# A gated state-space and attention kernel: score, maxima and convolution tiles of the second half drawn from three PSUM tiles in turn, with a new list of steps and edits to head, passage and tail

## The chip, the cores and the metric

The kernel runs on one core of a Trainium2 chip. The metric is the device time of one execution in microseconds (us); before the change the median of three runs is 784.46 us (779.76 to 787.62).

## What is computed

Input `x` is 2048 x 448. The output mixes two branches by a gate per row:

```python
g = sigmoid((x * gate_w).sum(-1, keepdims=True))
out = g * a + (1 - g) * b
# a: state-space convolution; 448 channels, 256 complex states each
A = -exp(log_A_real) + 1j * A_imag;  dt = exp(log_dt)
K = 2 * einsum("dn,dnl->dl", (C_real + 1j * C_imag) * dt[:, None], exp(A * dt * pos)).real
a = irfft(rfft(x, 4096) * rfft(K, 4096))[:2048] + x * D_skip
# b: 16 heads of 28 columns, 4 segments of 512 rows, causal softmax inside a segment
p = softmax(q @ k.T * scale + mask)
o = sigmoid(beta) * (phi(q) @ M) / (phi(q) @ z) + (1 - sigmoid(beta)) * (p @ v)
M = M + phi(k).T @ v;  z = z + phi(k).sum()      # after each segment
b = o @ wo
```

## The kernel before

**First half (to about 429 us).** `prepare_params` (the head) turns the state parameters into decays and phases per step. VectorE and ScalarE work on tiles of 112 x 1024; `parts` splits a result into three bf16 parts `sp`, which go by DMA to the DRAM tensors `SD` and `SP`, from where `load_decay` and `load_phase` bring them back as weights `lh` for TensorE. `first_half` then makes the kernel `K` in 56 rounds: phases by matmul (`ps_arg`), sines on ScalarE, products `X` and `Y` on VectorE, sums by matmul (`ps_k`), copied to `kb`. Between the rounds a generator, `Feed`, places pieces of `project` (queries, keys and values in high and low parts, written to the DRAM tensors `QD`, `KD`, `VD`; the memory `M`; weights `w` read back from `WD`) and of `transform_u` (first stage of the transform of `x`, written to `GU`). `feed.fill(n)` places n pieces of `transform_u` at once; one such call stands just before the last sums.

**Passage (428.9 to 461.8 us).** In `second_half`, eight rounds of `transform_k` take the first stage of the transform of `K` (PSUM tiles `w` and `c`, written to `GK`); between them stand fillers and the first steps of the maxima. `k.load(i)` loads queries and keys of unit i, 512 KB each.

**List of steps (461.8 to 760 us).** The string `PLAN` gives the order of the rest, one letter a step; TensorE, VectorE and ScalarE keep this order, each in its own queue. There are 16 units (segment, group of four heads). The letters that matter here:

- `m`: one of six steps of `maxima`: row maxima of the scores of two heads, by matmul into a PSUM tile and VectorE's reductions `jk`. `t` ends a unit's maxima: transposed, negated, written into a spare row of the queries.
- `w`: one of six steps of `weigh`: scores of two heads into a PSUM tile, exponential on ScalarE into `PT`. `p`: GpSimd masks `PT`. `V`, `v`: `values`, p times v, into the PSUM tile `pv`.
- `c`: a step of `convolve`: second stage of the transform of `K` (`transform`, emptied by ScalarE into `ks`), of `x` with the product on VectorE (`product`: two operations `pr`), and the way back (`back`, emptied by ScalarE into `bs`).
- `s`: a step of `seg_end` (division, memory, output projection of a segment). `l`, `j`, `z`: load, join and last row block of `finish`. `d`: `divide`. `q`: load the next unit's queries and keys.
- a digit n: n filler matmuls (`turn_over`) on the constant tile `wz`, written to `pv`, whose result nobody reads.

PSUM in the second half holds one tile `m` and one `pv` of one bank each, and three tiles of two banks, `w`, `mx` and `c`, with a single buffer each. A score step always takes `w`, a maxima step `mx` (until the first `q`, `k.twin` lets them alternate with `c`), the convolution `c`, `z` takes `c` and `mx` by turns. A matmul has to wait until the engine that empties its tile is done with the last contents. Heads lie on row groups of 32 of TensorE's array (`tile_position=(32 * h, 0)`); a step has two of them, the neighbouring `m` and `w` the other two.

**Tail (760 us on).** `last_end` (L1226) projects the first head groups of the last segment into the tiles `w` and `mx`, runs the last values matmuls, divides, and projects the rest.

All matmuls stand at L1444, all transposes at L1447; ordered operations of VectorE and ScalarE at L1398; ordered loads of SP at L1460, and others at L1458 and L1468.

Of the kernel before, what the change touches and what calls it, by code (L numbers as in the profile page):

```python
# [23 lines left out]
D = 448  # L24
# [152 lines left out]
def prepare_params(nc, k, pool, early, gp):  # L177
# [87 lines left out]
    stt(d, g, 4.0 / TWO_PI, d, ALU.mult, ALU.subtract)  # L265
    nc.scalar.activation(d, d, AF.Abs, scale=0.25)
    ts(cr, cr, 0.0, 0.5, ALU.is_lt, ALU.mult)
    ts(ai, a, 32.0, None, ALU.mult)
# [5 lines left out]
    stt(ai, a, 0.5, ai, ALU.mult, ALU.add)  # L274
    ts(ci, ci, 0.0, -2.0, ALU.is_lt, ALU.mult)
    ts(ci, ci, 1.0, None, ALU.add)
    yield 2
# [30 lines left out]
def first_half(nc, k, gy, feed):  # L308
# [134 lines left out]
    for n in range(2 * NJ):  # L443
# [131 lines left out]
def convolve(nc, k, fp):  # L575
# [46 lines left out]
    def back(m):  # L622

        pt = k.ps("c")
# [28 lines left out]
def finish(nc, k, fp):  # L653
# [18 lines left out]
    def last(wc):  # L672
        ws = slice(2 * wc, 2 * wc + 2)
        py = k.ps(("c", "mx")[wc % 2])
        for w in range(2):
# [16 lines left out]
def project(nc, k, pp, early, filling):  # L692
# [31 lines left out]

    wsp = [pp.tile([128, 4, 2, 4, 32], F32R, name=f"wsp{i}") for i in range(2)]
    for w in wsp:
# [147 lines left out]
    for s in range(NSEG):  # L874
        if s > 0:
            yield -next(filling, 0.1)
        xh = pp.tile([128, 4, SEG], F32R, tag="xh", name="xh")
        xl = pp.tile([128, 4, SEG], F32R, tag="xl", name="xl")
        for t in range(4):
# [15 lines left out]
        if s == 0:  # L895
            split = weights()
            for _ in range(4):
                yield next(split)

# [20 lines left out]
        if s == 0:  # L920
            yield from values(s, xh, xl, range(4))
            for x_ in split:
                yield -0.3
                k.turn_over(k.ps("m"), 3)
                yield 0.6
            yield from rest_of(plain)
        for i in range(0, len(units), 2):
# [27 lines left out]
            yield 0.1  # L955
        if s == 3:
            yield from rest_of(plain)
    yield from remember()
# [5 lines left out]
    k.gates()  # L964
    yield 0.1


def attend(nc, k, ap):
# [11 lines left out]

    Q, K, W, Vs, pvss = {}, {}, {}, {}, {}
    last = {}

    def load(i):
        if i >= 16:
            return
        s, hg = divmod(i, 4)
        for t, T, src in (("q", Q, k.QD), ("k", K, k.KD)):
            T[i] = ap.tile([128, 2, SEG], F32R, tag=t, name=t + "u", bufs=4)
            x = k.dma(T[i].bitcast(F32), src[s, hg])  # L990
        if i < 4:
            k.mark(x)

# [9 lines left out]
    def maxima(i):  # L1003
# [36 lines left out]
    def weigh(i):  # L1040

        q, kk = Q.pop(i), K.pop(i)
        W[i] = PT = ap.tile([128, 4, 1280], F32, tag="PT", name="PT", bufs=2)
        for b, hp in STEPS:
            pt = k.ps("w")
            for kt, o, n in PLACES[b]:
                for a, (x, y) in enumerate(((0, 0), (1, 0), (0, 1))):
                    for z in range(2):
                        h = 2 * hp + z
                        r = slice(32 * h, 32 * h + 32)  # L1050
                        k.mm(
                            pt[:, z, o : o + n], kk[r, x, 128 * kt : 128 * kt + 128], q[r, y, 128 * kt :],
                            start=(a == 0), stop=(a == 2), tile_position=(32 * h, 0),
                        )
            n = 512 if b < 2 else 256
            act(
                PT[:, 2 * hp : 2 * hp + 2, 512 * b : 512 * b + n], pt[:, :, :n], AF.Exp, scale=SCALE
            )
            yield

# [151 lines left out]
    def divide(hg):  # L1212
# [6 lines left out]
        for h in range(2):  # L1219
# [4 lines left out]
            x = v.tensor_tensor(o[:, c], o[:, c], am[3][:, hg, c], ALU.add)  # L1224

    def last_end(step, vals):  # L1226

        s = 3
        yds, pos = [], []
# [4 lines left out]
        for t in ("w", "mx"):  # L1234
            pt = k.ps(t)
            pos += [pt[:, 0, :D], pt[:, 1, :D]]

        def project(h, hgs):
            for t in (2 * h, 2 * h + 1):
                out_mm(s, t, pos[t], hgs)  # L1240
# [6 lines left out]
        for h in range(2):  # L1247
            project(h, [2, 3] if h else [3])
            for t in (2 * h, 2 * h + 1):
                po, yd, i = pos[t], yds[t], 12 + t  # L1250
# [4 lines left out]
    k.load, k.maxima, k.weigh, k.values, k.seg_end = load, maxima, weigh, values, seg_end  # L1255
    k.divide, k.last_end, k.skip_last = divide, last_end, skip_last


def second_half(nc, k, ap, tp, fp, fin):
# [9 lines left out]
    attend(nc, k, ap)  # L1269
    k.load(0)  # L1270


# [8 lines left out]
    k.twin = k.turn = False  # L1281
    first = transform_k(nc, k, tp)
    ms = {i: k.maxima(i) for i in range(16)}
    for r in range(8):
        step(first)
        turn_over(3)
        if r == 1:
            k.load(1)
        for _ in range((0, 1, 2, 1, 2, 1, 1, 0)[r]):
            step(ms[0])  # L1290
        if r >= 6:
            step(ms[1])
        if r == 6:
            k.load(2)
# [20 lines left out]
    def run(c):  # L1315
# [11 lines left out]
        elif c == "w":  # L1327
            if n % 6 == 0:
                w = k.weigh(n // 6)
            step(w)  # L1330
        elif c == "p":
            step(w)
# [13 lines left out]
        elif c == "d":  # L1346
            k.divide(n)
        elif c == "c":
            step(cv)
# [38 lines left out]
def gated_mix(ctx, tc, k):  # L1388
# [131 lines left out]
    def more_constants():  # L1520
        const("s1k", k.c_s1k, [128, 2, 128])
        const("fc", k.c_f, [128, 64])
        const("den", k.c_den, [128, 128])
        sel = const("self", k.c_sel, [40, 128])
# [35 lines left out]
    def psum_pool(stack, shapes):  # L1560
# [6 lines left out]
        k.ps = ps  # L1567

    kst = ExitStack()
    with ExitStack() as st:  # L1570
# [59 lines left out]
    with ExitStack() as st:  # L1630
        psum_pool(
            st,
            {"m": ([128, 512], 1), "pv": ([128, 512], 1)} | {t: ([128, 2, 512], 1) for t in ("mx", "w", "c")},
        )
        ap = pool(st, "ap", "right")
        k.mk = ap.tile([128, 512], F32, name="mk")
        nc.sync.dma_start(k.mk, k.c_mk)
        k.dbc = ap.tile([128, D], F32, name="dbc")
# [46 lines left out]
```

## Time and profile before

| | |
|---|---|
| runs | 784.46 us median (779.76 to 787.62, three runs) |
| profiled execution | 782.84 us, its span 781.1 us |
| TensorE (PE) busy | 686.6 us, 88% |
| VectorE (DVE), ScalarE (ACT), GpSimd (POOL) busy | 579.4, 503.9, 157.0 us |
| mean granted TensorE clock | 0.976 |
| DMA | 158.69 MB, 203 GB/s over the span |

In the profile, PE is a matmul and PEld a weight load, which may run under the matmul before it. A busy PE is not a PE at its peak, since matmuls are pipelined and their ends modelled. A wait is put down to what came last. "issue" is time in which an engine waited for nothing that the profile shows. A row of a group ends with the idle time before its instructions and what ended it.

### The profile page before, as it was taken

Reading aid. Unit: us, or ns where it says so; the run is one execution under the profiler, and the core shown is the slowest. Engines: PE = TensorE matmul, PEld = TensorE weight load, DVE = VectorE, ACT = ScalarE, POOL = GpSimd, SP = SyncE. Lnnn points to the kernel's source line nnn. Section 1 sums busy time; section 2 is a strip of 40 time slices with the busy share of each in tenths; the row PEclk is TensorE's granted clock in tenths of the full one; section 3 lists DMA queues with packets and bytes.
Section 4 is the critical chain, followed back from the end, with each engine's and each line's share of the span. In section 5 each row is a group of like instructions: output and inputs, shape, how many; then the busy total and the mean of one; then the engine's idle time right before and its main releaser. Section 6 shows DMA issues by size and latency. Waiting matters only on the chain.

```text
span 781.1 us, 18982 instructions
## 1 busy us (share of the span) xinstructions
PE 686.6 (88%) x7640; PEld 377.5 (48%) x7640; DVE 579.4 (74%) x1151; ACT 503.9 (65%) x614; POOL 157.0 (20%) x193
## 2 busy tenths in 40 slices
PE   1676998899888998989998899899999899998997
PEld 1353565566545765556564444443444344444443
DVE  8878588869888878899678665667647584674574
ACT  4878689879998899999887224555524533551230
POOL 4404301110111011100110002224112412341110
PEclk9989999999999999999999999999999899999999
DMA  8627774234464335651465997998857977766793
GB/s 204 183 63 232 234 239 155 85 107 149 148 220 134 106 101 182 198 167 55 143 208 183 362 335 258 277 312 284 278 196 246 309 251 246 223 217 212 187 320 118
DMA packets 94989, 158.69 MB, mean 203 GB/s; under 512 B 24398, under 2 KB 62470, under 8 KB 94902
## 3 DMA queue, kind: packets, MB, share of 16 engines
q1 hardware_dynamic: 90950, 154.78, 61.1%
q10 hardware_dynamic: 3072, 1.84, 0.8%
q8 instruction: 60, 0.98, 0.6%
q0 software_dynamic: 880, 0.87, 0.4%
q14 instruction: 27, 0.22, 0.1%
HBM read 89.25 MB, written 60.24 MB: 191 GB/s over the span
## 4 chain that ended last, share of the span: by engine, by line
PE 56%; DVE 14%; ACT 11%; DMA 4%; issue 4%; SPq 1%; DVEq 0%; ACTq 0%
PE ps_m L1444 20%; PE ps_c L1444 8%; PE ps_w L1444 6%; PE ps_pv L1444 6%; PE ps_arg L1444 5%; PE ps_k L1444 5%; ACT cs L1398 5%; PE ps_mx L1444 4%; DVE jk L1398 3%; DVE Y L401 2%; DVE cs L381 2%; DMA ks<-ks 2%; PE ps_m L1447 2%; ACT PT L1398 1%; DVE X L397 1%
## 5 line engine op out<-in xcount | busy, mean ns | idle before, releaser
L1398 ACT ACTIVATE PT<-ps_w 128x1024 f32<-128x1024 f32 (+1 forms) x96 | 84.6, 881 | 115.9 <-PE ps_w L1444 112.2
L1398 DVE CUSTOM_DVE_ANT_0 jk<-ps_mx,mk 128x128 f32<-128x128 f32 (+3 forms) x242 | 106.9, 488 | 59.0 <-PE ps_mx L1444 55.0
L358 POOL TENSOR_TENSOR EX<-EX,cab 128x1024 f32<-128x1024 f32 x28 | 53.5, 1912 | 293.5 <-ACT EX L1398 209.9
L1398 ACT ACTIVATE cs<-ps_arg 128x1024 f32<-128x1024 f32 x97 | 94.5, 1023 | 10.5 <-DVE cs L381 10.3
L1067 POOL TENSOR_SCALAR_AFFINE_SELECT PT<-PT 128x256 f32<-128x256 f32 (+1 forms) x96 | 47.5, 494 | 222.8 <-ACT PT L1398 222.8
L1444 PE MATMUL ps_w<-qu,ku 32*128 32x512 f32 (+3 forms) x768 | 86.1, 340 | 3.0 <-ACT PT L1398 2.5
L1444 PE MATMUL ps_m<-xh,w 128*128 128x512 f32 x224 | 79.1, 413 | 0.6 <-DMA w<-WD 0.5
L1444 PE MATMUL ps_k<-Y,X 128*32 128x64 f32 x3584 | 62.6, 222 | 15.2 <-DVE Y L402 15.1
L397 DVE TENSOR_TENSOR X<-EX,cs 128x1024 f32<-128x1024 f32 x56 | 69.2, 1236 | 5.3 <-ACT cs L1398 4.7
L1444 PEld LDWEIGHTS ps_k<-Y,X 128*32 128x32 f32 x3584 | 53.5, 111 | 40.7 <-DVE Y L402 29.1
L401 DVE TENSOR_TENSOR Y<-EY,cs 128x1024 f32<-128x1024 f32 x56 | 71.0, 1267 | 0.0
L1444 PEld LDWEIGHTS ps_w<-qu,ku 32*128 32x128 f32 x768 | 59.4, 184 | 22.6 <-ACT PT L1398 12.2
L1398 ACT ACTIVATE cs<-cs,bhp 128x1024 f32<-128x1024 f32 x56 | 64.3, 1149 | 1.4
L1398 ACT ACTIVATE EY<-ps_arg 128x1024 f32<-128x1024 f32 x52 | 52.3, 1037 | 5.7 <-PE ps_arg L1444 5.4
L1444 PE MATMUL ps_mx<-ku,qu 32*128 32x128 f32 (+3 forms) x242 | 42.5, 385 | 10.0 <-DVE mx L1398 9.6
L1444 PEld LDWEIGHTS ps_m<-xh,w 128*128 128x128 f32 x224 | 42.0, 187 | 18.3 <-issue 8.2
L1444 PE MATMUL ps_m<-xl,w 128*128 128x512 f32 x128 | 50.1, 391 | 0.0
L403 DVE SCALAR_TENSOR_TENSOR Y<-EY,cs 128x512 f32<-128x512 f32 x56 | 38.7, 692 | 15.3 <-ACT cs L1398 14.2
L1444 PE MATMUL ps_arg<-ct,lh 64*128 64x512 bf16 x224 | 43.9, 380 | 4.9 <-ACT cs L1398 3.0
L1444 PEld LDWEIGHTS <-lh 64*128 64x128 bf16 x392 | 21.9, 94 | 49.9 <-issue 35.2
L1444 PEld LDWEIGHTS ps_mx<-ku,qu 32*128 32x128 f32 x242 | 20.6, 184 | 51.2 <-DVE mx L1398 29.8
L1444 PE MATMUL ps_pv<-wz 128*128 128x512 bf16 x143 | 42.9, 389 | 0.5
(220 smaller groups left out, 1308.4 us busy)
## 6 DMA issues: line engine op xcount, KB each, us to landing
w<-WD SPq DMA_DIRECT2D x32, 448.0 KB
qu<-QD SPq DMA_DIRECT2D x16, 512.0 KB
ku<-KD SPq DMA_DIRECT2D x16, 512.0 KB
GU<-gs SPq DMA_DIRECT2D x32, 224.0 KB
GK<-gs SPq DMA_DIRECT2D x8, 896.0 KB
gk<-GK SPq DMA_DIRECT2D x16, 448.0 KB
gu<-GU SPq DMA_DIRECT2D x16, 448.0 KB
ks<-ks SPq DMA_DIRECT2D x32, 224.0 KB
```

The lines of the kernel that those rows point to most:

```text
L358: nc.gpsimd.tensor_tensor(o, o, cab, ALU.mult)
L381: v.tensor_scalar(t[:, 0].rearrange("p w t c -> p t w c").bitcast(I32), pv.bitcast(I32), 0x7FFFFFFF, None, ALU.bitwise_and)
L397: v.tensor_tensor(X, ex, t[:, :, 0], ALU.mult)
L401: v.tensor_tensor(Y[:, :, :, :32], lo, y[:, :, :, ::-1], ALU.mult)
L403: v.scalar_tensor_tensor(Y[:, 1, :, 32:], ey[:, :, 32:], -1.0, y[:, 1], ALU.mult, ALU.mult)
L1067: nc.gpsimd.affine_select(sl, sl, pat, ALU.is_ge, 0.0, base=0, channel_multiplier=-1)
L1398: x = op(*args, **kw)
L1444: tc.keep_in_program_order(nc.tensor.matmul(*args, **kw))
L1447: tc.keep_in_program_order(nc.tensor.transpose(*args))
```

## The change

- **Rotation.** A command `R` at the start of `PLAN` sets `k.rotates`. From there every request for one of the three two-bank tiles, by `weigh`, `maxima`, `convolve`, `finish` or the last projection, gets the next of `w`, `mx`, `c` in turn. (`y`, which skips one, is defined and not used.)
- **Four heads.** A command `u` runs a block of `weigh` for both head pairs at once, with interleaved matmuls, two PSUM tiles and then two exponentials. It stands three times in the list, for two `w` each.
- **List.** The same steps in slightly other places; the digits sum to 128 instead of 119.
- **Passage.** Queries and keys of a unit share one tile, in a pool `qk` of four slots that lives through the whole kernel. The first half's `v1`, `wsp`, `xh` and `xl` are the first users of these slots (`xh` and `xl` are now allocated once and not per segment). `k.load(0)` and `k.load(1)` are issued in the first half, behind a weight load of the last segment; `k.load(2)` in round 1 of the passage. The mask `mk` is loaded among the constants of the first half. One maxima step stands before the first round, and then one a round. `feed.fill(4)` before the last sums is `feed.fill(2)`.
- **Head.** Six buffers instead of three for `sp`. The absolute value of `d` on VectorE, as max(-d, d), without the factor 0.25; other factors follow.
- **Tail.** The last values matmuls come first; then the projection in six pieces, one ahead of the division, five behind it.

```diff
-            sp = pool.tile(W, BF16, tag="sp", name="sp", bufs=3)
+            sp = pool.tile(W, BF16, tag="sp", name="sp", bufs=6)
...
-    nc.scalar.activation(d, d, AF.Abs, scale=0.25)
-    ts(cr, cr, 0.0, 0.5, ALU.is_lt, ALU.mult)
+    stt(d, d, -1.0, d, ALU.mult, ALU.max)
+    ts(cr, cr, 0.0, 2.0, ALU.is_lt, ALU.mult)
...
-    feed.fill(4)
+    feed.fill(2)
     sums(2 * NJ - 1)
...
-        pt = k.ps("c")
+        pt = k.ps(k.rot("c"))
...
-    V = pp.tile([128, 4, 16, 32], F32, name="v1")
+    V = k.qk.tile([128, 4, 16, 32], F32, tag="qk", name="v1", bufs=4)
+    split = k.qk.tile([128, 2, 4, 2, 4, 32], F32R, tag="qk", name="wsp", bufs=4)
+    xh = k.qk.tile([128, 4, SEG], F32R, tag="qk", name="xh", bufs=4)
+    xl = k.qk.tile([128, 4, SEG], F32R, tag="qk", name="xl", bufs=4)
...
         if s == 3:
+            with k.issue_after(holds[4]):
+                k.load(0)
+                k.load(1)
             yield from rest_of(plain)
...
+        both = k.qk.tile([128, 2, 2, SEG], F32R, tag="qk", name="qku", bufs=4)
+        for t, (T, src) in enumerate(((Q, k.QD), (K, k.KD))):
+            T[i] = both[:, t]
+            x = k.dma(T[i].bitcast(F32), src[s, hg])
...
-            pt = k.ps("c" if k.twin and k.turn else "mx")
+            pt = k.ps(k.rot("c" if k.twin and k.turn else "mx"))
...
+        for b in range(3):
+            for hps in ((0, 1),) if k.four else ((0,), (1,)):
+                pts = {hp: k.ps(k.rot("w")) for hp in hps}
+                for kt, o, n in PLACES[b]:
+                    for a, (x, y) in enumerate(((0, 0), (1, 0), (0, 1))):
+                        for hp in hps:
+                            for z in range(2):
...
+    def piece():
+
+        h, hg = divmod(pieces["done"], 3)
+        pieces["done"] += 1
+        if hg == 0:
+            pt = k.ps(k.rot(("c", "mx")[h]))
+            pieces[h] = [pt[:, 0, :D], pt[:, 1, :D]]
+        for t in (2 * h, 2 * h + 1):
+            out_mm(3, t, pieces[h][t % 2], [hg])
...
-        project(0, range(2))
-        step(vals)
-        project(0, [2])
-        divide(3)
-        project(1, range(2))
...
+        step(vals)
+        if pieces["done"] < 6:
+            piece()
+        divide(3)
+        while pieces["done"] < 6:
+            piece()
...
+    def rot(tag):
+        if not k.rotates:
+            return tag
+        tags[0] += 1
+        return ("w", "mx", "c")[tags[0] % 3]
...
+    for _ in range(1):
+        step(ms[0])
     for r in range(8):
         step(first)
-        turn_over(3)
+        turn_over((3, 3, 3, 3, 3, 3, 3, 3)[r])
+        for _ in range((1, 1, 1, 1, 1, 1, 1, 0)[r]):
+            step(ms[0])
+        for _ in range((0, 0, 0, 0, 0, 0, 1, 1)[r]):
+            step(ms[1])
         if r == 1:
-            k.load(1)
-        for _ in range((0, 1, 2, 1, 2, 1, 1, 0)[r]):
-            step(ms[0])
-        if r >= 6:
-            step(ms[1])
-        if r == 6:
             k.load(2)
...
+        elif c == "u":
+            if at["w"] % 6 == 0:
+                w = k.weigh(at["w"] // 6)
+            at["w"] += 2
+            k.four = True
+            step(w)
+            k.four = False
+        elif c == "R":
+            k.rotates = not k.rotates
...
 PLAN = """
-4m12mm2m33wm21swm2wmt3swms4wms13wsmp2qmwsvmwcmwscmtw2smwcm5w
-sscpoVqmwsvmwtcmwcsmws1mwscwmscpVqmwsvmwtcmwcsmwmscwms3wscpV
-qmwsvmwtecmwsc4mws11mwsc1mwscpVqmwscvmw2tmwscmwscmwsmwscpVmq
-wsvcmw1tmwscmwscmws1mwscpVqmwsvmcw2tms1wc1mwscmwsmwsc1pVqmwc
-vmwt2semwscmws2cmws1mwcspVqmwscvmwtcsmw2m1wscmw33scmwspV2qmw
-scvmwtcwkmsmwckmswcs1kmwkspVqmwcsvkmwtckmw1s1kmwscmwscwm1spV
-3qwmscvmwtemcwsm3wscmwscmwspV2Cfqmwslvmwt21ss2lm2ws13lsmw2s4
-slmwsslmws4spVjjjjjjqw2swtvwsd2z2lwzjlsjwszwslzdpVqwszvwzswz
-swdzwsw4spV
+R4m12mm1m33wm21swm2wmt3swms4wms3wsmp2qmwsvmwcmwscmtw2smwcm5w
+sscspoVqmwvmwtcsmw2cmws1mwscwm1scpVqmwsvmwtcmwcsmw2mscwms2ws
+cpVqmwsvmwtecmwsc4mws111mwscmw1scpVqmwsvmwc2tmwscmwscmws2mws
+cpVmwsqvcmw1tmuscmscmws1mwsc2pVqmwsvmcw2tmswc21mwscmwsmwsc1p
+Vqmwcvmwt1semwscmws21cmws1mwcspVqmw3svmwtcsmw2cmwscmw3s3cmws
+pVqmwscvmwtcwkmsmwckmsucs1kmkspVqmwcsvkmwtckmws2kmwscmwscwm1
+spV3qwsmcvmw1metcw1ms3wsmcwscmwpV1Cfqsmswlvmwt11ss2lm2ws13ls
+1mw2s4slmwsslmws4spVjjjjjjq2swtvwswd2z2lwzjlsjwszwslzdpVqusz
+vzswzswdwsw4zspV
 """
...
-            {"m": ([128, 512], 1), "pv": ([128, 512], 1)} | {t: ([128, 2, 512], 1) for t in ("mx", "w", "c")},
+            {"m": ([128, 512], 1), "pv": ([128, 512], 1)} | {t: ([128, 2, 512], 1) for t in ("w", "mx", "c")},
```

More of the change, by code (lines that the diff above doesn't have):

```diff
@@ L723, in rows @@
         return [(t[64 * h : 64 * h + 64], src[384:]) for h in range(2)]
-    wsp = [pp.tile([128, 4, 2, 4, 32], F32R, name=f"wsp{i}") for i in range(2)]
+    wsp = [split[:, i] for i in range(2)]
     for w in wsp:
@@ L895, in project @@
         if s == 0:
-            split = weights()
+            parts = weights()
             for _ in range(4):
-                yield next(split)
+                yield next(parts)
         if s == 0:
@@ L921, in project @@
             yield from values(s, xh, xl, range(4))
-            for x_ in split:
+            for x_ in parts:
                 yield -0.3
@@ L965, in project, with loads, load @@
     yield 0.1
+def loads(k):
+    Q, K = k.Q, k.K = {}, {}
+    def load(i):
+        if i >= 16:
+            return
+        s, hg = divmod(i, 4)
+        both = k.qk.tile([128, 2, 2, SEG], F32R, tag="qk", name="qku", bufs=4)
+        for t, (T, src) in enumerate(((Q, k.QD), (K, k.KD))):
+            T[i] = both[:, t]
+            x = k.dma(T[i].bitcast(F32), src[s, hg])
+        if i < 4:
+            k.mark(x)
+    k.load = load
 def attend(nc, k, ap):
@@ L979, in load_wo @@
         k.ldma(k.dbc, k.D_skip.unsqueeze(0).broadcast_to([128, D]))
-    Q, K, W, Vs, pvss = {}, {}, {}, {}, {}
+    Q, K, load = k.Q, k.K, k.load
+    W, Vs, pvss = {}, {}, {}
     last = {}
[L984 to L992, printed above, removed]
     STEPS = [(b, hp) for b in range(3) for hp in range(2)]
@@ L1043, in weigh @@
         W[i] = PT = ap.tile([128, 4, 1280], F32, tag="PT", name="PT", bufs=2)
[L1044 to L1059, printed above, removed]
+        for b in range(3):
[5 more added lines that the diff above has]
+                            for z in range(2):
+                                h = 2 * hp + z
+                                r = slice(32 * h, 32 * h + 32)
+                                k.mm(
+                                    pts[hp][:, z, o : o + n], kk[r, x, 128 * kt : 128 * kt + 128],
+                                    q[r, y, 128 * kt :],
+                                    start=(a == 0), stop=(a == 2), tile_position=(32 * h, 0),
+                                )
+                n = 512 if b < 2 else 256
+                for hp in hps:
+                    act(
+                        PT[:, 2 * hp : 2 * hp + 2, 512 * b : 512 * b + n], pts[hp][:, :, :n], AF.Exp, scale=SCALE
+                    )
+                yield
         for hp in range(2):
@@ L1224, in divide @@
             x = v.tensor_tensor(o[:, c], o[:, c], am[3][:, hg, c], ALU.add)
+    pieces = {"done": 0}
+    def piece():
[6 more added lines that the diff above has]
+            out_mm(3, t, pieces[h][t % 2], [hg])
     def last_end(step, vals):
         s = 3
-        yds, pos = [], []
+        yds = []
         for t in range(4):
@@ L1254, in attend @@
     k.load_wo = load_wo
-    k.load, k.maxima, k.weigh, k.values, k.seg_end = load, maxima, weigh, values, seg_end
-    k.divide, k.last_end, k.skip_last = divide, last_end, skip_last
+    k.maxima, k.weigh, k.values, k.seg_end = maxima, weigh, values, seg_end
+    k.divide, k.last_end, k.skip_last, k.piece = divide, last_end, skip_last, piece
 def second_half(nc, k, ap, tp, fp, fin):
@@ L1347, in run @@
             k.divide(n)
+        elif c == "x":
+            k.piece()
         elif c == "c":
@@ L1522, in more_constants @@
         const("fc", k.c_f, [128, 64])
+        k.mk = cp.tile([128, 512], F32, name="mk")
+        k.bulk(k.mk, k.c_mk)
         const("den", k.c_den, [128, 128])
@@ L1567, in psum_pool @@
         k.ps = ps
+    k.qk = pool(ctx, "qk", "right")
+    loads(k)
     kst = ExitStack()
```

30 lines of the change are left out of this document (12 added, 18 removed).

## The prediction

> **What bounds the kernel now.** I read the page first, then the busy time by stretches, the waits of TensorE and of its weight loader in the stage of the change, and last the chain and the timeline at the four places that the diff touches. The page:
>
> ```profile
> span 781.1 us, 18982 instructions
> ...
> PE 686.6 (88%) x7640; PEld 377.5 (48%) x7640; DVE 579.4 (74%) x1151; ACT 503.9 (65%) x614; POOL 157.0 (20%) x193
> ...
> PE 56%; DVE 14%; ACT 11%; DMA 4%; issue 4%; SPq 1%; DVEq 0%; ACTq 0%
> ```
>
> TensorE is busiest and has most of the chain. By stretches (the passage, the written list of steps, the tail; columns: length, then busy time of PE, PEld, DVE, ACT, POOL, granted clock, DMA share, GB/s):
>
> ```profile
> 428.90:461.80 32.90, 29.18 (x203) 13.55 (x203) 22.83 (x73) 7.60 (x9) 1.63 (x2) 1.00 0.91 334
> 461.80:760.00 298.20, 278.15 (x2291) 129.10 (x2291) 189.74 (x575) 131.60 (x173) 73.10 (x126) 0.98 0.79 259
> 760.00:781.10 21.10, 16.75 (x70) 7.29 (x70) 10.88 (x15) 1.19 (x2) 0.65 (x2) 1.00 0.35 110
> ```
>
> The list takes 298.2 us; DVE and ACT have 108 and 167 us to spare in it, PE idles 20.1. What these 20 us wait for, of PE and of its weight loader in 461.8 to 760 (total, times, longest):
>
> ```profile
> PE ps_mx L1444 <- DVE mx L1398: 6.9, 15, 0.9
> PE ps_w L1444 <- ACT PT L1398: 2.5, 6, 0.7
> PE ps_c L1444 <- DVE pr L1398: 2.1, 3, 1.0
> ...
> PEld ps_mx L1444 <- DVE mx L1398: 25.6, 35, 1.6
> PEld ps_pv L1444 <- issue: 22.6, 71, 1.4
> ...
> PEld ps_w L1444 <- ACT PT L1398: 12.2, 21, 1.1
> ```
>
> The tiles of the maxima and of the weights are refilled before VectorE or ScalarE has emptied them: 56 waits of the loader, 37.8 us. A gap that no tile causes is 22.6 / 71 = 0.32 us, so 56 x 0.32 = 18 us are ordinary and about 20 are stall; PE's rows show 6.9 + 2.5 = 9.4 of it, since the ends of earlier matmuls cover the rest.
>
> **The rotation.** Today a score step always takes `w`, a maxima step `mx`, the convolution `c`. After R the three tiles go round over all requests, so each comes back after exactly three. The list has 96 score steps, 88 maxima steps and 48 of the convolution in both versions (three `u` count for two steps each), 8 last row blocks and 2 projection tiles: 242 requests, one every 298.2 / 242 = 1.23 us, and only their places differ. So `w` comes back after 242 / 96 = 2.5 requests on average today, `mx` after 2.75, `c` after 5. Where the list runs "mwsc" the distance is three already and nothing changes; where it runs "mws mws" it is two and becomes three. An emptying takes
>
> ```profile
> L1398 ACT ACTIVATE PT<-ps_w 128x1024 f32<-128x1024 f32 x64 | 65.5, 1024 | 69.8 <-PE ps_w L1444 66.4 <-DMA cb<-in_c_bk 1.8 <-POOL PT L1067 1.1
> ...
> L1398 DVE CUSTOM_DVE_ANT_0 jk<-ps_mx,mk 128x512 f32<-128x512 f32 x62 | 40.3, 687 | 28.3 <-PE ps_mx L1444 27.3 <-PE ps_w L1444 0.8
> ...
> L1398 DVE TENSOR_TENSOR pr<-ps_c,ks 128x896 f32<-128x896 f32 x32 | 33.4, 1085 | 7.4 <-PE ps_c L1444 4.7 <-issue 1.8 <-ACT mn L1398 0.7
> ```
>
> 1.02 us for weights, 2 x 0.69 for a wide maxima step, 2 x 1.09 for a product, plus DVE's queue. Another 1.23 us of room is more than most waits of the two rows (25.6 / 35 = 0.73 and 12.2 / 21 = 0.58 us), but only where the distance grows, and the product's 2.2 us, harmless at a distance of five, now stands in everybody's way. Bounds: nothing, or all 20 us; I take a third, **6.5 us**, nearer to PE's own 9.4.
>
> The Trainium skill (TensorE: Matmul & The Clock Gate, "A second HAM failure mode: psum-queue depth-cycling") speaks against this: a kernel that cycled through PSUM banks made TensorE idle so often for moments that its clock kept dropping. The trace has 0.98 of the clock over the list, with the tiles cycling already; that row and the rule differ so far.
>
> **Filler matmuls.** The digits of the list sum to 119 before and 128 after. One costs 1.04 / 4 = 0.26 us (tail fence below), nine 2.3; some will stand in waits, so **+1.8 us** (0 to 2.3).
>
> **Four heads at once.** `u` runs a score block for both head pairs, interleaved, so four row groups of 32 work together. Its price from the transform of the kernel sums, which already uses four, and from pairs at 512 and 256 columns:
>
> ```profile
> 429.36 0.57 PE L1444 MATMUL ps_w<-kb,s1k 32*128 32x448 f32 x2
> ...
> 429.40 0.54 PE L1444 MATMUL ps_c<-kb,s1k 32*128 32x448 f32 x2
> ...
> 429.74 0.57 PE L1444 MATMUL ps_w<-kb,s1k 32*128 32x448 f32 x2
> ```
> ```profile
> 749.13 0.96 PE L1444 MATMUL ps_w<-qu,ku 32*128 32x512 f32 x6
> ...
> 751.67 1.08 PE L1444 MATMUL ps_w<-qu,ku 32*128 32x384 f32 x12
> ...
> 758.05 0.62 PE L1444 MATMUL ps_w<-qu,ku 32*128 32x256 f32 x6
> ```
>
> Four start every 0.38 us, so the second pair is free. The three `u` stand at the 512, the 384+128 and the 256 block: 0.96 + 1.08 + 0.62 = 2.7 us at most. A maxima step next to a score step uses the other two row groups, though, and loses that company; nothing at least. I take **1.0 us**.
>
> The Trainium skill (TensorEngine Tiling (Array Packing), "PSUM Bottleneck") says that packing speeds the matmuls and not the emptying of PSUM. Two exponentials of 1024 ns then follow one block: by that rule this term would be 0.
>
> **Head.** `d`'s absolute value moves from ScalarE to VectorE, and six instead of three buffers hold the bf16 parts.
>
> ```profile
> 28.33 1.22 DVE L210 SCALAR_TENSOR_TENSOR pin_d<-pin_g,pin_d 112x1024 f32<-112x1024 f32 x1
> ...
> 34.64 1.06 ACT L266 ACTIVATE pin_d<-pin_d 112x1024 f32<-112x1024 f32 x1 [0.24 <-issue]
> ...
> 35.73 1.22 DVE L210 TENSOR_TENSOR pin_cr<-pin_d,pin_cr 112x1024 f32<-112x1024 f32 x1 [2.99 <-ACT pin_d L266]
> ...
> 53.81 1.06 ACT L1419 ACTIVATE sp<-pin_d 112x1024 bf16<-112x1024 f32 x1 [1.91 <-DVE pin_mn L210]
> ...
> 58.03 0.96 PE L1447 MATMUL ps_m<-ident,pin_mx 112*128 112x112 f32 x8 [0.92 <-DVE gz L857]
> ...
> 60.07 0.61 PE L1444 MATMUL ps_arg<-ct,lh 64*128 64x512 bf16 x2 [1.07 <-DMA lh<-SP]
> ```
>
> VectorE waited 2.99 us for ScalarE and now spends 1.22 (as in the first row) itself: 1.8 earlier. The last part waited 1.91, which I read as its buffer: together 3.7 us on the way to the load that the first phase matmul (60.07) waits for. The transposes ahead of it, which need `pin_mx` from the same VectorE, allow about 2.7. Bounds 0 and 2.7; **2.0**. The other edits of the head only change scale factors. One fill step less before the last sums moves PE's work past them and not out: 0.
>
> **Passage.** Loads of the first two query and key pairs move from its start into the end of the first half, 4 x 512 KB, and the mask with them; a maxima step goes ahead of the transform.
>
> ```profile
> 428.91 0.64 PE ps_w L1444 x2
> ...
> 434.57 0.50 PE ps_mx L1444 x2
> ...
> 461.86 0.43 PE ps_w L1444 x2
> ```
>
> The first maxima matmul comes at 434.57, 5.7 us after the transform's first, and the first score at 461.86. In between PE idles 32.9 - 29.2 = 3.7 us; the maxima steps are now one a round instead of up to two, which evens out VectorE, and 2 MB leave a stage at 334 GB/s. Filler count there falls by two (31 to 29, counted above). The gain is at most 3.7; **2.0**. Against it: on SP the loads stand behind a weight load of the projection and before the next ones, and the projection once waited
>
> ```profile
> 91.47 5.29 DMA w<-WD
> ```
>
> 5.3 us for such a load: the loss at worst. Behind them on SP stand the stores of key halves and the next weights, which the projection's matmuls wait for. 2 MB at 334 GB/s take 6.3 us; with two weight buffers I expect little of it. The slots that these loads take are those of the first half's `v1` and `wsp`, whose last readers are done by then, so no wait is added there: 0, or again the 5.3 if not.
>
> **Tail.** The first projections go behind the last values matmuls, one last row block goes behind the fillers:
>
> ```profile
> 759.36 0.62 PE L1444 MATMUL ps_w<-qu,ku 32*128 32x256 f32 x6 [0.69 <-ACT PT L1398]
> ...
> 759.91 1.04 PE L1444 MATMUL ps_pv<-wz 128*128 128x512 bf16 x4
> ...
> 760.78 3.17 PE L1444 MATMUL ps_w<-wo,pvs 128*128 128x448 f32 x8
> ...
> 763.88 2.36 PE L1444 MATMUL ps_pv<-PT,V 128*32 128x512 f32 x32
> ```
>
> The values start earlier, but the work that stood before them follows, and PE has hardly a gap: only the 0.69 us wait goes (up to 3.2, the projections' length, if VectorE's division ends it); **0.7**.
>
> **Sum.** 2.0 + 2.0 + 6.5 + 1.0 + 0.7 - 1.8 = **10.4 us**. The profiled execution took 782.84 us (span 781.1, 1.7 around it), which gives 772.4. The median of the runs shown is 784.46, 1.6 above it; against that the forecast is **774.1 us**, 1.3% less. A measurement of this kernel can tell about 1% from no change (its three runs span 1.0%).
>
> **Rivals.**
> 1. *The stalls only change their tile.* For: PE takes everything in order, and the "mwsc" stretches keep their distance; the searched list has more fillers, not fewer. Against: ACT and DVE have over 100 us to spare. Then head, passage and tail less fillers remain, 4.7 - 1.8 = 2.9, so 781.6.
> 2. *All of it goes.* The whole 20 us: 13.5 more than forecast, 760.6. For: waits shorter than the room gained. Against: DVE's products.
> 3. *The early loads hold up the projection.* 5.3 lost and the passage's 2.0 not won: 781.4.
> 4. *Slower: the product becomes everybody's wait.* From the point where VectorE's maxima (1.4 us) and product (2.2 us) together outlast three requests (3.7 us), each of 16 product steps holds the score step behind it. At 1.0 us each (the longest wait of PE on `pr`) it costs 16 us in place of the 6.5: 774.1 + 22.5 = 796.6. For: 3.6 is nearly there, and any third operation on VectorE passes it. Against: long steps (values, fillers) stand between many requests.
> 5. *Slower: the clock.* If the whole list ran at 0.91, as single stretches of it do,
>
> ```profile
> 480.00:500.00 20.00, 18.50 (x173) 8.70 (x171) 12.37 (x44) 9.58 (x14) 4.45 (x9) 0.91 0.93 274
> ```
>
> it would cost 278 x (0.98 / 0.91 - 1) = 21 us: 784.46 + 21 - 2.9 = about 803.
>
> ```profile
> PEclk9989999999999999999999999999999899999999
> ```
>
> The page's row shows no trend towards it. (The rule of the Trainium skill cited above, TensorE: Matmul & The Clock Gate, would bring it about.)
>
> **How the numbers follow.** Forecast 0.45 (of it 0.36 past 1%, that is under 776.6), rival 1 0.25, 2 0.13, 3 0.07, 4 0.08, 5 0.02. Faster 0.36 + 0.13 = 0.49; slower 0.10; within 1% 0.09 + 0.25 + 0.07 = 0.41. Forecast's own range: 768 to 779. The range that holds 8 in 10 takes in rivals 1 and 3 and half of 2: 764 to 786.
>
> **What would show it.** Right: loader waits of the three tiles in the list fall from 37.8 us to about 25, PE's idle time from 20 to 14; the first score matmul near 458; the first phase matmul near 58; `u` blocks at 0.6 to 1.1 us for 12 or 24 matmuls. Wrong: waits on `pr` and `PT` that grow by what those on `mx` lose, a `w<-WD` wait near 400 us, or a list as long as before with PE less idle because of fillers.

## The result, and the profile after

The changed kernel takes 771.65 us (median of four runs, 768.53 to 775.0); the kernel before took 785.34 us on the same chip. The ratio is 0.986, its 95% interval 0.982 to 0.991: 1.4% faster. The forecast was 774.1 us.

The profiled execution of after took 775.0 us, the longest of the four; its span is 773.3. From its page:

```profile
span 773.3 us, 19022 instructions
...
PE 685.5 (89%) x7649; PEld 376.8 (49%) x7649; DVE 585.5 (76%) x1152; ACT 502.1 (65%) x613; POOL 155.4 (20%) x193
...
PE 56%; DVE 13%; ACT 12%; DMA 5%; issue 4%; DVEq 0%; SPq 0%; POOL 0%; ACTq 0%; POOLq 0%
```

PE does the same work in a span 7.8 us shorter, and nothing has taken its place on the chain. By stretches (passage, list, tail; columns as in the prediction):

```profile
429.60:458.00 28.40, 27.94 (x183) 12.60 (x183) 19.31 (x53) 7.60 (x9) 0.63 (x1) 0.94 0.82 307
458.00:755.00 297.00, 281.26 (x2335) 129.92 (x2338) 195.38 (x597) 131.92 (x174) 73.10 (x127) 0.98 0.79 261
755.00:773.30 18.30, 14.01 (x54) 6.77 (x46) 10.22 (x15) 0.60 (x1) 0.00 (x0) 1.00 0.40 125
```

In the list PE idles 297 - 281.3 = 15.7 us (20 before, 14 forecast) at the same clock of 0.98. The waits of the weight loader in 458 to 752 (total, times, longest), three rotating tiles, three reasons:

```profile
PEld ps_mx L1483 <- DVE mx L1437: 7.9, 14, 1.3
PEld ps_c L1483 <- DVE mx L1437: 6.0, 10, 0.7
PEld ps_w L1483 <- DVE mx L1437: 5.8, 11, 0.7
...
PEld ps_mx L1483 <- ACT PT L1437: 1.8, 3, 0.7
PEld ps_mx L1483 <- DVE pr L1437: 1.5, 2, 1.0
PEld ps_c L1483 <- DVE pr L1437: 1.2, 1, 1.2
...
PEld ps_w L1483 <- DVE pr L1437: 0.6, 2, 0.4
...
PEld ps_w L1483 <- ACT PT L1437: 0.4, 1, 0.4
PEld ps_c L1483 <- ACT PT L1437: 0.2, 1, 0.2
```

The maxima cost 7.9 + 6.0 + 5.8 = 19.7 us where one tile cost 25.6; the weights 2.4 where they cost 12.2. Together 37.8 has become 22.1; the forecast said about 25. The product, feared as everybody's wait, holds 1.5 + 1.2 + 0.6 = 3.3 us. PE's own waits on the maxima and the weights, 9.4 us in the kernel before, are down to 0.5. Its idle time fell by less, since other waits grew: those of the loader on the convolution's emptyings by ScalarE, `ks` and `bs`, went from 4.1 to 6.3 us.

One trace against one trace says little here, since executions of one kernel differ by 1%. So I cut each trace of this study at the same five events and compare lengths: A, from the start of the 12th copy `kb` of the first half to the 14th and last; B, from there to the first exponential `PT`; C, from there to the last `PT` (the list); D, from there to the first of the last two `yd` (the tail). All in us, with the median of the runs beside the ratio to the kernel before. The experiments ran on three chips, on which the kernel before took 784.45 us (e1 to e4), 781.97 (e5 to e8) and 781.54 (e9 to e12); each ratio is to the kernel before on the same chip, so kernels of different chips are compared by ratio:

| kernel | A | B | C | D | median, ratio [95%] |
|---|---|---|---|---|---|
| before | 50.1 | 35.0 | 297.2 | 16.9 | 785.34 |
| after | 52.2 | 33.6 | 289.8 | 17.5 | 771.65, 0.986 [0.982, 0.991] |
| after, once more (e12) | 51.5 | 32.0 | 289.4 | 18.0 | 772.78, 0.988 [0.982, 0.993] |
| e1: old list, no rotation | 52.5 | 34.5 | 299.6 | 16.6 | 783.69, 0.999 [0.995, 1.003] |
| e2: old list, rotation | 53.1 | 32.2 | 293.1 | 17.2 | 774.91, 0.990 [0.985, 0.995] |
| e3: new list, no rotation | 53.5 | 34.2 | 302.4 | 18.0 | 788.93, 1.006 [1.003, 1.009] |
| e9: before with rotation alone | 50.2 | 35.5 | 295.1 | 23.1 | 783.83, 1.002 [0.998, 1.005] |
| e4: late loads | 50.9 | 32.0 | 290.0 | 17.5 | 770.56, 0.982 [0.978, 0.985] |
| e5: late loads, old head | 49.8 | 32.0 | 288.2 | 17.5 | 769.49, 0.986 [0.983, 0.990] |
| e6: late loads, no four heads | 49.8 | 32.0 | 290.5 | 17.5 | 767.90, 0.983 [0.980, 0.986] |
| e7: late loads, 14 fillers less | 50.0 | 33.3 | 284.2 | 17.7 | 767.50, 0.984 [0.981, 0.988] |
| e8: late loads, four fill steps | 51.2 | 33.1 | 289.8 | 17.5 | 772.03, 0.987 [0.984, 0.991] |
| e10: late loads, old list | 50.3 | 33.6 | 293.2 | 17.2 | 774.27, 0.991 [0.988, 0.995] |
| e11: e6 and e7 together | 49.8 | 32.0 | 287.8 | 17.5 | 768.38, 0.982 [0.978, 0.987] |

For after, C and D come from these rows of ScalarE and VectorE (start, duration): 751.53 - 461.71 = 289.8 and 769.05 - 751.53 = 17.5.

```profile
461.71 1.02 ACT L1437 ACTIVATE PT<-ps_c 128x1024 f32<-128x1024 f32 x1 [7.13 <-PE ps_c L1483]
...
751.53 0.59 ACT L1437 ACTIVATE PT<-ps_c 128x512 f32<-128x512 f32 x1
```
```profile
769.05 1.28 DVE L1437 SCALAR_TENSOR_TENSOR yd<-ps_c,ogt,yd 128x448 f32<-128x448 f32 x2 [0.23 <-PE ps_c L1483]
```

No kernel here leaves out or changes part of the computation; fillers are read by nobody.

### The profile page after: what moved, and what is told of

Read it like the earlier page. It is cut to its first block, busy times and chain, and to the rows that moved or that the text cites. A ratio compares the mean times of both kernels' runs of the same rounds, so it can differ in the third digit from the quotient of the medians.

```text
span 773.3 us, 19022 instructions
## 1 busy us (share of the span) xinstructions
PE 685.5 (89%) x7649; PEld 376.8 (49%) x7649; DVE 585.5 (76%) x1152; ACT 502.1 (65%) x613; POOL 155.4 (20%) x193
## 4 chain that ended last, share of the span: by engine, by line
PE 56%; DVE 13%; ACT 12%; DMA 5%; issue 4%; DVEq 0%; SPq 0%; POOL 0%; ACTq 0%; POOLq 0%
PE ps_m L1483 19%; PE ps_pv L1483 7%; PE ps_c L1483 7%; PE ps_w L1483 7%; PE ps_mx L1483 6%; ACT cs L1437 6%; PE ps_arg L1483 5%; PE ps_k L1483 4%; DVE Y L401 2%; DVE cs L381 2%; PE ps_m L1486 1%; DVE jk L1437 1%; DMA ks<-ks 1%; DVE X L397 1%; DVE Y L402 1%
## 5 line engine op out<-in xcount | busy, mean ns | idle before, releaser
L358 POOL TENSOR_TENSOR EX<-EX,cab 128x1024 f32<-128x1024 f32 x28 | 53.5, 1912 | 294.0 <-ACT EX L1437 211.2
L1437 DVE CUSTOM_DVE_ANT_0 jk<-ps_mx,mk 128x512 f32<-128x512 f32 (+3 forms) x94 | 42.0, 494 | 22.5 <-PE ps_mx L1483 21.3
L1437 ACT ACTIVATE PT<-ps_c 128x1024 f32<-128x1024 f32 (+1 forms) x30 | 26.9, 895 | 45.8 <-PE ps_c L1483 42.5
L1437 ACT ACTIVATE PT<-ps_mx 128x1024 f32<-128x1024 f32 (+1 forms) x37 | 31.0, 838 | 36.0 <-PE ps_mx L1483 35.2
L1437 DVE CUSTOM_DVE_ANT_0 jk<-ps_w,mk 128x256 f32<-128x256 f32 (+3 forms) x86 | 36.9, 475 | 19.5 <-PE ps_w L1483 18.6
L1483 PE MATMUL ps_mx<-qku 32*128 32x256 f32 (+3 forms) x376 | 48.7, 353 | 3.2 <-ACT ks L1437 1.5
L1483 PEld LDWEIGHTS <-lh 64*128 64x128 bf16 x392 | 22.1, 94 | 50.9 <-issue 37.1
L1483 PE MATMUL ps_pv<-wz 128*128 128x512 bf16 x152 | 45.7, 387 | 0.6
L1437 DVE CUSTOM_DVE_ANT_0 jk<-ps_c,mk 128x512 f32<-128x512 f32 (+3 forms) x76 | 33.7, 490 | 14.4 <-PE ps_c L1483 11.6
```

What stands on the lines that cost most here:

```text
L358: nc.gpsimd.tensor_tensor(o, o, cab, ALU.mult)
L1437: x = op(*args, **kw)
L1483: tc.keep_in_program_order(nc.tensor.matmul(*args, **kw))
```

## The experiments

### Rotation and list, each alone (e1, e2, e3)

All three are the changed kernel with head, passage and tail as changed. e1 and e2 take the old list, e3 the new one with each `u` written as two `w`:

```diff
 PLAN = """
-R4m12mm1m33wm21swm2wmt3swms4wms3wsmp2qmwsv...
+4m12mm2m33wm21swm2wmt3swms4wms13wsmp2qmwsv...      e1 (e2: the same with R ahead)
+4m12mm1m33wm21swm2wmt3swms4wms3wsmp2qmwsv...       e3
```

> The changed kernel with the old list of steps and no rotation; head, passage, tail and the shared pool stay as changed. Theory A (the three tiles in turn take away stalls of the list): only head, passage and tail are left, about 3 us less than before, 782. Theory B (the gain lies in head, passage and tail, the list only follows): nearly all of it stays, 772 to 774.

> The changed kernel with the old list of steps, the three tiles in turn from its start. Theory A: 5 to 7 us below the same without rotation, about 776, since waits for VectorE's and ScalarE's emptying fall whatever the list; the waits of the weight loader on the exponentials fall from 12 to under 4 us. Theory C (the rotation pays only with a list made for it, since a product's emptying now stands in everybody's way): no faster than without rotation, about 782 or more, with waits on pr that grow by what the others lose.

> The changed kernel with the new list, R taken out and each u replaced by two w. Theory A: the stalls on single-buffered tiles are back and nine more fillers stand in the way: 780 to 784. Theory D (the new places of the steps do it, not the tiles): 772 to 775.

Measured 783.69, 774.91 and 788.93 us, on one chip. On the old list the rotation takes off 783.69 - 774.91 = 8.8 us. On the new one the ratio goes from 1.006 to 0.986 and 0.988, about 15 us. The new list without rotation is 5.2 us slower than the old one, so it is no gain by itself; with rotation 0.986 and 0.988 against 0.990 (e2) does not separate the two lists (e10 below does). And e1's interval, 0.995 to 1.003, leaves head, passage and tail together at most 3.6 us without the rotation: they are not the main source of the gain, but the 3 us of theory A are not excluded.

The waits agree. With the new list and fixed tiles (e3) the loader waits in 458 to 758 as before and more:

```profile
PEld ps_mx L1483 <- DVE mx L1437: 27.8, 39, 1.2
...
PEld ps_w L1483 <- ACT PT L1437: 14.5, 21, 1.6
```

and with the old list under rotation (e2, 458 to 752) they are nearly those of after, 8.3 + 6.5 + 4.7 = 19.5:

```profile
PEld ps_mx L1483 <- DVE mx L1437: 8.3, 14, 0.8
PEld ps_c L1483 <- DVE mx L1437: 6.5, 11, 0.8
PEld ps_w L1483 <- DVE mx L1437: 4.7, 8, 0.8
```

### The rotation and nothing else (e9)

If the rotation gives 8.8 us and the rest nothing, the rotation in the kernel before should give 8.8 as well. e9 is the kernel before with `rot` around the six requests for these tiles, and:

```diff
 PLAN = """
-4m12mm2m33wm21swm2wmt3swms4wms13wsmp2qmwsvmwcmwscmtw2smwcm5w
+R4m12mm2m33wm21swm2wmt3swms4wms13wsmp2qmwsvmwcmwscmtw2smwcm5w
```

> The kernel before with the rotation switched on at the start of its own list, and nothing else of the change. Theory R (the rotation is the whole gain on the old list, and head, passage and tail are worth nothing on the sum): as the kernel with the old list and the rotation, 774.9 us, ratio 0.988 to 0.992. Rival S (head, passage and tail are worth some 3 us that the early loads hide): 777 to 778, ratio 0.993. By the prediction's term for the rotation alone: 784.46 - 6.5 = 778, ratio 0.992.

Measured 783.83 us, ratio 1.002 to the 781.54 of this chip: all three expectations fail. The table says where it went: C falls by 2.1 us, and D grows by 6.2. In the list the loader waits on the maxima as in e2 (8.3 + 6.4 + 4.7 = 19.4), so the stalls went here too; why C falls by 2.1 only, where e2 has 6.5 less than e1, no run shows. Here is PE at the end of e9:

```profile
754.13 1.04 PE L1455 MATMUL ps_pv<-wz 128*128 128x512 bf16 x4
758.79 6.04 PE L1455 MATMUL ps_mx<-wo,pvs 128*128 128x448 f32 x8 [3.63 <-DVE rest L1409]
764.76 1.71 PE L1455 MATMUL ps_pv<-PT,V 128*32 128x512 f32 x16
```

VectorE's `rest`, for which the projection waits, is the emptying of the last row block's tile, queued behind the reciprocals of a division:

```profile
754.74 1.75 DVE L1409 RECIPROCAL rcb<-ps_m 128x256 f32<-128x256 f32 x1
756.52 0.48 DVE L1409 SCALAR_TENSOR_TENSOR pvs<-pvs,omg,rcb 128x256 f32<-128x256 f32 x1
757.04 0.43 DVE L1409 TENSOR_TENSOR pvs<-pvs,am 128x256 f32<-128x256 f32 x1
757.38 1.27 DVE L1409 SCALAR_TENSOR_TENSOR rest<-ps_mx,gt,rest 128x448 f32<-128x448 f32 x2
```

In the kernel before, the first projections wrote to `w`, which ScalarE had emptied. In turn comes `mx`, the tile of the last row block. PE stands still for 3.63 us with the values matmuls behind it, and then works at half speed: eight projections take 6.04 us instead of 3.17. The granted clock in the seventh column (after length, PE, PEld, DVE, ACT, POOL) shows it:

```profile
754.00:758.00 4.00, 1.17 (x12) 0.31 (x4) 3.90 (x7) 1.09 (x2) 1.23 (x2) 0.95 0.05 19
758.00:762.00 4.00, 3.21 (x5) 1.60 (x6) 0.65 (x2) 0.00 (x0) 0.00 (x0) 0.50 0.44 115
762.00:766.00 4.00, 4.00 (x21) 1.37 (x23) 0.00 (x0) 0.00 (x0) 0.00 (x0) 0.70 0.62 177
```

With the changed tail (e2) the values matmuls, which need only `pv`, go first and cover that emptying; 1.02 us of the wait is left and D is 17.2:

```profile
752.85 2.36 PE L1483 MATMUL ps_pv<-PT,V 128*32 128x512 f32 x32
...
756.23 1.02 PE L1483 MATMUL ps_mx<-wo,pvs 128*128 128x448 f32 x2 [1.02 <-DVE rest L1437]
```

So the tail edit is worth 23.1 - 17.2 = 5.9 us with the rotation and next to nothing without it (16.9 before, 16.6 in e1). The old tail under rotation has one trace; the twelve with the changed tail lie between 16.6 and 18.0.

### The early loads (e4, e10, e12)

In the trace of after, SP issues the four loads of queries and keys at 385.2 to 387.8, and DMA is full (last two columns: share, GB/s):

```profile
385.00:390.00 5.00, 4.93 (x140) 2.87 (x140) 5.00 (x8) 4.78 (x7) 0.00 (x0) 1.00 1.01 352
390.00:395.00 5.00, 5.00 (x89) 3.76 (x82) 4.89 (x6) 2.79 (x4) 0.00 (x0) 1.00 1.01 352
395.00:400.00 5.00, 3.25 (x15) 1.85 (x14) 3.32 (x8) 4.96 (x8) 0.00 (x0) 1.00 0.53 199
```

What is late there are stores of 256 KB and 8 KB, `AM` and `DM`, issued behind the loads. The chain of what ended last has the store of `AM` for 6.95 us; ScalarE's next exponentials `e` use the buffer that these stores read, and wait; then PE waits for ScalarE:

```profile
389.85 6.95 DMA AM<-am
```
```profile
394.88 1.28 ACT L1437 ACT_TABLE_LOAD   x1 [2.17 <-DMA DM<-am]
```
```profile
399.23 0.39 PE L1483 MATMUL ps_arg<-ce,lh 64*128 64x512 bf16 x2 [1.75 <-ACT EY L1437]
```

This wait of ScalarE is there in all five traces with early loads, 2.1 to 3.0 us, and in none of the nine others. The 13th copy of the sums comes 404.55 - 375.94 = 28.6 us behind the 12th, 26.0 in the kernel before (403.70 - 377.69):

```profile
375.94 1.08 DVE L424 COPY kb<-ps_k 128x512 f32<-128x512 f32 x1 [0.69 <-PE ps_k L1483]
404.55 1.02 DVE L424 COPY kb<-ps_k 128x512 f32<-128x512 f32 x1
```

e4 issues the loads behind the projection's last pieces, at 402 to 406 us; e10 does it with the old list under rotation; e12 is the changed kernel again.

```diff
+            yield from rest_of(plain)
             with k.issue_after(holds[4]):
                 k.load(0)
                 k.load(1)
-            yield from rest_of(plain)
```

> The changed kernel, with the loads of the first two query and key pairs issued behind the last key units of the projection instead of before them. Theory E (the early 2 MB delay the stores of the memory term, whose buffer the next exponentials need, and so cost the first half 2 to 3 us, all that the head won): the last copy of sums comes about 2.5 us earlier, near 425.5, the ACT wait on the memory stores near 395 us is gone, and the whole is 1 to 2.5 us faster, 769 to 770.5. Rival F (that wait is slack): the last copy of sums stays near 428, and the passage begins its maxima later: 772 to 774.

> The changed kernel with the loads of the first two units behind the projection's last pieces, and with the old list under the rotation. Theory L (the new list is worth about 3 us under the rotation, late loads 1 to 4): 771 to 774, ratio 0.985 to 0.990. Rival T (the order of steps no longer matters once the tiles rotate): the same as late loads with the new list, ratio 0.9815, 769 us.

> The changed kernel as it is, on the same chip as the three above. Early loads cost 1 to 4 us by the copy of the block sums that is late by 2.6 us: ratio 0.984 to 0.988. If they cost nothing, the ratio is that of late loads, 0.9815.

The wait is gone in e4: 400.86 - 374.75 = 26.1 us between the two copies, and the last copy comes at 425.60 us instead of 428.13, as theory E said.

```profile
374.75 1.08 DVE L424 COPY kb<-ps_k 128x512 f32<-128x512 f32 x1 [0.69 <-PE ps_k L1483]
400.86 1.05 DVE L424 COPY kb<-ps_k 128x512 f32<-128x512 f32 x1
```

Over all traces this distance is 27.8 to 29.8 us in the five with early loads and 26.0 to 26.4 in the nine others. Column A, one copy later, still has some 2 us of it (51.5 to 53.5 against 49.8 to 51.2). In the medians such a gain is not resolved: 0.982 for e4 against 0.986 and 0.988 with early loads, but 0.991 (e10) against 0.990 (e2). e12 came out where a cost of the early loads was expected (0.988), with an interval (from 0.982) that overlaps e4's (to 0.985). So the loss is shown in the trace, with its place; its worth in the end stays within the measurement. Whether the order in SP's queue or the full DMA delays the stores, no run separates.

e10 also prices the list under rotation: 0.991 against 0.982 for e4, with intervals that do not overlap, and C 293.2 against 290.0. That is theory L, a little above its range. The order of steps still matters once the tiles rotate.

### Single terms on top of late loads (e5 to e8, e11)

```diff
-    stt(d, d, -1.0, d, ALU.mult, ALU.max)                            e5: the head as before
+    nc.scalar.activation(d, d, AF.Abs, scale=0.25)                   (other factors follow)
-            sp = pool.tile(W, BF16, tag="sp", name="sp", bufs=6)
+            sp = pool.tile(W, BF16, tag="sp", name="sp", bufs=3)
-...mw1tmuscmscm...wckmsucs1kmk...pVquszvz...                         e6: each u as ww
+...mw1tmwwscmscm...wckmswwcs1kmk...pVqwwszvz...
-...mwtcsmw2cmws1mwscwm1scp...                                        e7: 114 fillers, not 128
+...mwtcsmwcmws1mwscwmscp...
-    feed.fill(2)                                                     e8
+    feed.fill(4)
```

> Late loads, with the old head (absolute value on ScalarE, three buffers for the parts). Theory G (the head's 2 to 3 us are on the path, once the early loads no longer eat them): first sine at 62.6 instead of 59.2, the last copy of sums near 428 instead of 425.6, the whole 2 to 3 us slower than with late loads, 773. Rival H (the first half takes up the head's gain in later waits anyway): the last copy of sums within 0.7 us of 425.6, the whole the same.

> Late loads, with each of the three u replaced by two w. The forecast's term: about 1 us slower, with the three blocks 0.6 to 1.0 us longer on PE each. Rival (two exponentials behind one block, and the maxima step that loses its company, take it back): no difference within the noise, 770.5.

> Late loads, with 14 of the 128 fillers of the list taken out, at places where the old list has none or fewer. The forecast's term (0.26 us each, most of it in the way): 2.5 to 3.6 us faster, 767 to 768. Rival I (they stand in waits, or keep the clock up): no faster, 770 or more, and the granted clock of the list no higher than 0.98.

> Late loads, with four pieces of the first transform ahead of the last sums as before the change. The forecast's term is 0. Rival J (with two ahead, PE idles before the last sums and the clock drops in the passage in some executions): the transform of the kernel sums runs without a stretch at 0.86 of the clock, last copy of sums up to 1 us later, the whole 0 to 2 us faster.

> Late loads, the four-head blocks taken apart into two ordinary steps each, and 14 of the list's 128 fillers left out (nobody reads what they compute). Theory F (fillers cost 0.26 us each where they don't stand in waits, the four-head block nothing): 0 to 3.6 us less than late loads alone, 765 to 769 us, ratio 0.978 to 0.982. Rival G (the fillers stand in waits and keep the clock up): 769 to 772, ratio 0.983 to 0.986.

Ratios 0.986, 0.983, 0.984, 0.987 and 0.982, in that order, all with intervals that overlap e4's 0.978 to 0.985. e11 falls between its two theories (0.982 and 0.983). No edit here is worth more than this measurement can tell. The traces add something for four of them. With the old head (e5) the last copy of the sums comes at 425.87 us, within 0.3 of e4's 425.60, as rival H said. The four-head block gives C 290.0 with it (e4) and 290.5 without (e6): nothing. With fewer fillers C is 284.2 (e7) and 287.8 (e11); the six traces of the new list with rotation and all its fillers lie between 288.2 and 290.5, so only e7 is clearly below them, and its granted clock over the list is 0.99 where theirs is 0.98. The medians of one chip, 767.50 us for e7 against 767.90 for e6, show no gain. And in e8, with four fill steps as before the change, the clock falls at the start of the passage all the same (0.90, seventh column), so the two fill steps less, which rival J named, are not its cause:

```profile
428.00:440.00 12.00, 11.71 (x86) 5.52 (x80) 8.27 (x26) 3.67 (x4) 0.00 (x0) 0.90 0.59 196
```

The ratios of the six kernels with late loads and the new list, 0.982 to 0.987, lie around and below the two of the change itself (0.986, 0.988); singly none is separated from it.

## Why the prediction was right, and which of its steps were not

**The rotation (6.5 us)** was the right mechanism, and its size depends on the rest. On the old list C falls by 6.5 us in the changed kernel (299.6 to 293.1, e1 to e2; 8.8 in the medians) and by 2.1 in the kernel before (297.2 to 295.1, e9), on the new list by some 13 (302.4 to 289.8). These are single traces. I took a third of the 20 us because the product would stand in everybody's way. It held the loader 3.3 us in all, and the stalls on the weights went almost wholly. Rival 4 was close to its condition, 3.6 us of VectorE's work against 3.7 for three requests, but did not come about; whether the long steps between the requests are the reason, no run tried. Rival 1 is excluded by the waits, which shrank, and rival 2 by the 15.7 us of idle time that are left.

What I missed is that the term has a condition outside the list. In the old tail the rotation hands the projection a tile that VectorE empties late, and 6.2 us go there (e9). I had costed the tail edit in the kernel before, where `w` is free, at 0.7; there it is worth 0.3 (16.9 to 16.6), but its worth is 5.9 us as soon as the tiles rotate. **A sum of edits, each costed alone in the kernel before, hid that one of them makes another possible.**

**The list (no term of its own, but +1.8 for its fillers).** Under the rotation it gives 3 us of C (293.1 to 289.8, 293.2 to 290.0), fillers and all: their price is more than met by better places. All of PE's fillers in after, those of the passage among them, cost 0.6 us of idle time and 45.7 of busy time:

```profile
L1483 PE MATMUL ps_pv<-wz 128*128 128x512 bf16 x152 | 45.7, 387 | 0.6
```

**Four heads (1.0 us).** The price per block was nearly right (forecast 0.6 to 1.1 us; the three took 1.21, 0.55 and 0.89), but the gain did not come. The last `u`:

```profile
739.15 0.50 PE L1483 MATMUL ps_w<-qku 32*128 32x512 f32 x2
739.15 0.50 PE L1483 MATMUL ps_mx<-qku 32*128 32x512 f32 x2
...
740.04 1.72 PE L1483 MATMUL ps_c<-bt,fc 128*64 128x448 f32 x8
```

Twelve matmuls in 0.89 us, where six took 0.96. But e6 shows no gain from it: 0.983 without `u` and 0.982 with it. The Trainium skill (TensorEngine Tiling (Array Packing), "PSUM Bottleneck") says that packing does not speed the emptying. The runs fit that, but a gain of 1 us would be too small to be told here, and no run tries the reason.

**Head (2.0 us): wrong.** The first phase matmul, forecast near 58, comes at 56.92 in after. But it does so with the old head as well, at 57.10 in e9 and 56.77 in e5:

```profile
56.92 0.80 PE L1483 MATMUL ps_arg<-ct,lh 64*128 64x512 bf16 x2 [0.29 <-DMA lh<-SP]
```
```profile
57.10 0.79 PE L1455 MATMUL ps_arg<-ct,lh 64*128 64x512 bf16 x2 [0.25 <-DMA lh<-SP]
```

The step that failed is the 2.99 us that VectorE waited for the absolute value. In e9, the same code, it is

```profile
34.72 1.22 DVE L210 TENSOR_TENSOR pin_cr<-pin_d,pin_cr 112x1024 f32<-112x1024 f32 x1 [1.52 <-ACT pin_d L266]
```

1.52, and 0.48 in e5:

```profile
34.33 1.23 DVE L210 TENSOR_TENSOR pin_cr<-pin_d,pin_cr 112x1024 f32<-112x1024 f32 x1 [0.48 <-ACT pin_d L266]
```

The 1.91 us that I read as a wait for a buffer are 0.28 and 0.27 in these two. The length of both waits belonged to that one execution, not to the program, and I counted a gain for taking them away. The 12th copy of the sums comes at 373.95 and 376.10 us with the old head (e9, e5) and at 373.86 to 376.69 in the eleven traces with the new one, so nothing is left of the head's 2.0.

**Passage (2.0 us): more than forecast, and mostly given back.** Where the clock is undisturbed, B is 32.0 to 32.2 us in six traces with the changed passage, and 35.0 and 35.5 in the two with the old: 3.2 us. In the other six the granted clock falls just at its start, as in after, and not in e4:

```profile
428.00:440.00 12.00, 10.82 (x69) 4.85 (x71) 8.72 (x24) 3.13 (x4) 0.00 (x0) 0.86 0.53 198
```
```profile
428.00:440.00 12.00, 11.79 (x96) 6.05 (x92) 9.65 (x30) 3.67 (x4) 0.00 (x0) 1.00 0.79 266
```

and B is 33.1 to 34.5. This drop, whose cause stays open and which neither trace of the old passage has, and the 2 us of the early loads take back most of the gain. The first score matmul (into `c` now, from which the first `PT` is read) came at 460.69 us instead of the forecast 458 (459.01 in e12, 456.57 in e4).

```profile
460.69 0.50 PE L1483 MATMUL ps_c<-qku 32*128 32x512 f32 x2
```

**Rival 3 (early loads).** The damage came near 400 us, as it said, but not through `w<-WD`, which I had named: through the stores queued behind the loads, and the buffer that ScalarE takes over from them. I had looked at who waits behind the loads for weights, and not at who waits for a store's source to come free.

**The clock (rival 5)** stayed at 0.98 over the list. The rule that spoke against the change (the Trainium skill, TensorE: Matmul & The Clock Gate, "A second HAM failure mode: psum-queue depth-cycling") is not borne out by these runs: under the rotation the list's clock is the same and its idle time smaller.

**The sum.** Forecast -10.4 us; the medians differ by 785.34 - 771.65 = 13.7, the two profiled executions by 7.9 at the start of the last `yd` (776.91 and 769.05). Of these 7.9, list and tail give 7.4 in C less 0.6 in D, 6.8 where I had 6.5 - 1.8 + 0.7 = 5.4, or 6.4 with the four heads. Head and passage give 1.1 where I had 4.0: the 12th copy comes 1.8 earlier, which e9 and e5 show to be the execution and not the head, A is 2.1 longer and B 1.4 shorter. The rest of the 13.7 is in no trace; after's profiled execution is the longest of its four. So the forecast's total owes something to luck: it lies between two measures that are 6 us apart, and its terms for head, four heads and early loads were wrong.

## What to carry to other kernels

When buffers are handed out in turn instead of by purpose, walk the whole program for the request that now gets a buffer whose reader is late; it may be far from the place that gains (here the last 25 us of the kernel), and the edit that reorders that place is part of the change, not a separate term. A wait of a few microseconds in one trace should be looked for in a second execution before its removal is counted. When a burst of loads is moved earlier, list the stores queued behind it and who takes over their source buffers.

## What the runs showed of the hardware

- Around the end of 3.63 us of idleness PE was granted 0.50 of its clock (758 to 762 us) and 0.70 in the next 4 us (e9), and with the slow matmuls behind it the stall of 3.6 us cost 6.2. That fits what the Trainium skill says (TensorE: Matmul & The Clock Gate, "HAM oscillation — how this bites in real kernels"): no idle gaps above about 3.4 us.
- With DMA at a share of 1.01 and 352 GB/s, a store of 256 KB issued behind 2 MB of loads took 6.95 us (6.6 to 7.3 in four traces with early loads), and ScalarE waited 2.1 to 3.0 us for the buffer.
- Executions of one program differ in the order of microseconds at fixed places: the first phase matmul at 60.07 us in before and 57.10 in e9, whose code up to there is the same.
